# Scores as four row tiles of the matrix array, four single PSUM banks and two pairs

## The chip, the cores and the metric

One core of one Trainium2 chip. TensorE (PE) multiplies matrices out of SBUF into PSUM, eight banks of 128 partitions by 512 fp32; ScalarE (ACT) evaluates functions, VectorE (DVE) does elementwise work and reductions, GpSimd (POOL) the rest, and SyncE (SP) issues most DMAs. The metric is the device time of one execution in microseconds (us); lower is better.

## The reference

Input `x` is 2048 tokens of 448 features. Two branches read it and a sigmoid gate mixes them, everything in fp32:

```python
def _A_ref(x, wq, wk, wv, wo):                 # 16 heads of 28, one shared key and value
    q = (x @ wq).reshape(B, S, H, Dh).transpose(0, 2, 1, 3)
    k = x @ wk
    v = x @ wv
    scores = jnp.einsum("bhqd,bkd->bhqk", q, k) * (Dh ** -0.5)
    p = _softmax(scores, axis=-1)
    o = jnp.einsum("bhqk,bkd->bhqd", p, v)
    return o.transpose(0, 2, 1, 3).reshape(B, S, H * Dh) @ wo

def _B_ref(x, w1, w2, w3, w4):
    h = _gelu(_layernorm(x) @ w1)
    ...                                        # four column groups shifted by +1, -1, +2, -2 tokens
    x1 = x + hs @ w2
    return x1 + _gelu(_layernorm(x1) @ w3) @ w4

g = _sigmoid((x * gate_w).sum(-1, keepdims=True))
return g * a + (1 - g) * b
```

## The kernel before

The order of every engine's queue is written out by hand (a manual schedule): each engine runs its instructions in program order and waits on semaphores. Three stages follow one another.

**Stage 1 and 2 (first 401 us).** Projections to queries, keys, values (`stage_q`, `stage_kv`; they go through the DRAM tensor `qd`), the token mixer (`stage_w1`, `stage_w2`) and the MLP (`w3_part`, `w4_part`), each product made of two or three fp32r products of a high and a low half. `split_k` (L334) builds the keys for the attention on POOL. The last MLP product of the last block is left to the attention stage (`w4_job`, L835).

**Stage 3, attention.** It runs over 16 units `u` (four blocks of 512 queries by four groups of four heads). A unit has 16 key tiles `kt` of 128 keys. For each `kt` and head `j`, one matmul (L901) makes the scores of 128 keys by 512 queries in one PSUM bank: its 98 contraction rows are three stacked products of 32 rows (high q with high k, low q with high k, high q with low k, so that the sum is nearly fp32) and two rows that subtract a bound on the maximum. ACT reads the bank, writes `p = exp(scale * scores)` to SBUF (L903). Seven banks rotate for the scores (`bank`), the eighth holds the values: `pv_group` (L863) multiplies four `p` tiles by `vext` (values and a column of ones, 32 columns), each head in its own 32 columns of the array (`tile_position=(0, 32 * j)`, a column tile), and sums over a unit's 16 key tiles in that bank. These value products come in seven visits a unit (`VISITS`, L880), of two or three key tiles each; 22 `p` tiles (`PB`) bridge the time between.

**Around it.** `max_part` (L206) takes the scores of 32 keys of the next unit in four small matmuls, DVE their maximum (L211); `max_end` puts it as rows beside the queries by four small DMAs. `q_rows` (L192) copies the halves of a later unit's queries into the 98-row layout by three DMAs. `sums_begin`, `recip` and `norm` divide a finished unit by its sums, which go through DRAM to be spread over partitions (L780, L789, L791, L796). `wo_job` (L805) multiplies the result by `wo`, three matmuls of 448 columns for each 128 tokens, and DVE adds it to the output (L824). `pump` (L852) issues one matmul of a job at written places between the scores. After the last unit a tail divides by way of transposes on PE and checks that all sums are in range; else a block `redo` (not taken) computes everything with full maxima.

Of the kernel before, what the change touches and what calls it, by code (L numbers as in the profile page):

```python
# [16 lines left out]
P = 128  # L17
S = 2048
D = 448
# [12 lines left out]
PB = 22  # L32
# [9 lines left out]
def gated_mix_kernel(  # L42
# [25 lines left out]
    identR = keep.tile([P, P], F32R, name="identR")  # L68
    nc.vector.tensor_copy(identR, ident)
    x1 = keep.tile([P, NT, D], F32, name="x1")  # L70
    kS = keep.tile([P, S], F32R, name="kS")
# [14 lines left out]
    nc.gpsimd.memset(f32(kS)[96:128, :], 1.0)  # L86
# [4 lines left out]
    def misc_tile(name):  # L91
        return psA.tile([P, 512], F32, tag="misc", bufs=1, name=name)

# [85 lines left out]
    qs_of = [None, None]  # L179

    def q_load(u, raw):
        b, g = divmod(u, NG)
        qr_of[u] = raw
        nc.sync.dma_start(raw[0:4 * DH], qd[g, 0:4 * DH, 512 * b:512 * b + 512])

    def q_split(u, qh, ql):
        qr = qr_of.pop(u)[0:4 * DH]
        qh_of[u], ql_of[u] = qh[0:4 * DH], ql[0:4 * DH]
        nc.vector.tensor_copy(qh_of[u], qr)
        nc.vector.tensor_sub(ql_of[u], qr, f32(qh_of[u]))  # L190

    def q_rows(u):  # L192
        q_of[u] = qs_of[u % 2]
        for r, part in enumerate((qh_of[u], ql_of[u], qh_of[u])):
            nc.sync.dma_start(f32(q_of[u])[32 * r:32 * r + DH], f32(part))

    NU = NB * NG
    q_of = {}
    qr_of, qh_of, ql_of = {}, {}, {}
    mx_of = {}  # L200
    mc_of = {}

    def max_tile(name):
        return psA.tile([P, 512], F32, tag="mx", bufs=1, name=name)

    def max_part(u, t, tile_of):  # L206
        if t == 0:
            mx_of[u] = late.tile([P, 4, 4], F32, tag="mr", bufs=2, name=f"mr_{u}")
        ps = tile_of(f"m_{u}_{t}")[:, 0:4 * MK].rearrange("p (j k) -> p j k", j=4)
        nc.tensor.matmul(ps, qh_of[u][:, t * P:(t + 1) * P], khd[0:4 * DH], start=True, stop=True)  # L210
        nc.vector.reduce_max(mx_of[u][:, :, t], ps, axis=AX.X)  # L211

    def max_full(u, tile_of):
        mr = late.tile([P, 4, 4], F32, tag="mr", bufs=2, name=f"mf_{u}")
        for j in range(4):
            for t in range(4):
                mk = late.tile([P, NB], F32, tag="mk", bufs=2, name=f"mk_{u}_{j}_{t}")
                for kb in range(NB):
                    ps = tile_of(f"mf_{u}_{j}_{t}_{kb}")
                    nc.tensor.matmul(ps, q_of[u][0:96, j, t * P:(t + 1) * P], kS[0:96, kb * 512:kb * 512 + 512],  # L220
                                     start=True, stop=True)
                    nc.vector.reduce_max(mk[:, kb:kb + 1], ps, axis=AX.X)
                nc.vector.reduce_max(mr[:, j, t:t + 1], mk, axis=AX.X)
        mx_of[u] = mr

    def max_end(u):
# [7 lines left out]
        for p in range(4):  # L234
            nc.sync.dma_start(f32(qs_of[u % 2])[96:98, :, :].rearrange("k j (t p q) -> k p (j t) q", p=4, q=32)[:, p],
                              mrow[32 * p:32 * p + 32, :])
# [4 lines left out]
    with tc.tile_pool(name="s1b", bufs=1) as s1b, \  # L241
# [80 lines left out]
        kf_of = {}  # L322

        def stage_kv(b):
            cols = slice(512 * b, 512 * b + 512)
            kf = s1b.tile([96, 512], F32, tag="kf", bufs=2, name=f"kf_{b}")
            for r in range(3):
                for g in range(2):
                    nc.sync.dma_start(kf[32 * r + 16 * g:32 * r + 16 * g + 16, :], qd[g, 4 * DH:P, cols])
            for g in range(2):  # L330
                nc.sync.dma_start(vT[32 * b + 16 * g:32 * b + 16 * g + 16, :], qd[2 + g, 4 * DH:P, cols])
            kf_of[b] = kf

        def split_k(b):  # L334
            cols = slice(512 * b, 512 * b + 512)
            kf = kf_of[b]
            nc.gpsimd.tensor_copy(kS[0:96, cols], kf)
            nc.gpsimd.tensor_tensor(kS[64:96, cols], kf[64:96, :], f32(kS)[64:96, cols], ALU.subtract)
# [207 lines left out]
        split_k(0)  # L546
# [14 lines left out]
        split_k(1)  # L561
# [3 lines left out]
        split_k(2)  # L565
# [4 lines left out]
        khd = late.tile([P, 4, MK], F32R, name="khd")  # L570
        qh0 = late.tile([P, 512], F32R, tag="qh0", bufs=1, name="qh0")
        qs_of[0] = late.tile([P, 4, 512], F32R, name="qs0")
# [8 lines left out]
        def load_w34(i, pool):  # L581
            w3h.append(pool.tile([P, 4, 2 * P], F32R, name=f"w3h_{i}"))
            w3l.append(pool.tile([P, 4, 2 * P], F32R, name=f"w3l_{i}"))
            last = late if 2 * i + 2 == NF else pool
            w4h.append(last.tile([P, 2, D], F32R, name=f"w4h_{i}"))
            w4l.append(last.tile([P, 2, D], F32R, name=f"w4l_{i}"))
# [46 lines left out]
        split_k(3)  # L633
# [10 lines left out]
    with tc.tile_pool(name="s2", bufs=1, reuse_waits="tile") as s2, \  # L644
# [5 lines left out]
        fills = [lambda t=t: max_part(0, t, max_tile if t % 2 else misc_tile) for t in range(4)]  # L650
# [6 lines left out]
        def w3_part(b, f):  # L657
# [3 lines left out]
            if (b, f) == (NB - 1, NF - 1):  # L661
                gh = late.tile([P, 512], F32R, tag="qh0", bufs=1, name="gh_late")
                gl = late.tile([P, 512], F32R, name="gl_late")
            else:
                gh = s2.tile([P, 512], F32R, tag="gh", bufs=3, name=f"gh_{b}_{f}")
                gl = s2.tile([P, 512], F32R, tag="gl", bufs=3, name=f"gl_{b}_{f}")
            gf = s2.tile([P, 512], F32, tag="gf", bufs=2, name=f"gf_{b}_{f}")
# [14 lines left out]
        for b in range(NB):  # L682
            acc = [ps2.tile([P, 512], F32, tag="acc", bufs=4, name=f"acc_{b}_{t}") for t in range(4)]
            gs = {}
            for f in range(NF):
# [24 lines left out]
                if b == 1 and f == 1:  # L710
                    for z in (khd, qs_of[0][0:96]):
                        nc.gpsimd.memset(f32(z), 0.0)
                    for j in range(4):
                        nc.sync.dma_start(f32(khd)[j:4 * DH:4, j, :], f32(kS)[0:DH, 0:MK])
                    q_load(0, s2a.tile([P, 512], F32, tag="xn", bufs=1, name="qr_0"))
                if b == 1 and f == 5:
                    q_split(0, qh0, s2.tile([P, 512], F32R, tag="gl", bufs=3, name="ql_0"))
                    q_rows(0)
# [9 lines left out]
            if b == NB - 1:  # L728
                last_g = gs[NF - 1]
# [9 lines left out]
    with tc.tile_pool(name="s3", bufs=1, reuse_waits="tile") as s3, \  # L739
            tc.tile_pool(name="ps3", bufs=1, space=PSUM, reuse_waits="tile") as ps3:  # L740
        woh = s3.tile([P, 4, D], F32R, name="woh")
        wol = s3.tile([P, 4, D], F32R, name="wol")

        banks = [mm_tile("bank_0"), mm_tile("bank_1"), misc_tile("bank_2")]
        banks += [ps3.tile([P, 512], F32, name=f"bank_{i}") for i in range(3, 7)]
# [6 lines left out]
        qs_of[1] = s3.tile([P, 4, 512], F32R, name="qs1")  # L752
        nc.gpsimd.memset(f32(qs_of[1])[0:96], 0.0)
        def q_fetch(u):
            if u < NU:
                q_load(u, s3.tile([P, 512], F32, tag="qr", bufs=1, name=f"qr_{u}"))

        def q_begin(u):
            q_split(u, s3.tile([P, 512], F32R, tag="qh", bufs=2, name=f"qh_{u}"),
                    s3.tile([P, 512], F32R, tag="ql", bufs=1, name=f"ql_{u}"))  # L760

        q_fetch(1)
        q_begin(1)
        q_rows(1)
        q_fetch(2)
# [10 lines left out]
        def sums_begin(u, pv):  # L776
            o = s3.tile([P, 512], F32, tag="o", bufs=2, name=f"o_{u}")
            nc.vector.tensor_copy(o, pv)  # L778
# [15 lines left out]
        def norm(u, o, rb):  # L794
            on = s3.tile([P, 512], F32, tag="onf", bufs=2, name=f"on_{u}")
            nc.vector.tensor_mul(on, o, rb)  # L796
            onh = s3.tile([P, 512], F32R, tag="onh", bufs=2, name=f"onh_{u}")
            onl = s3.tile([P, 512], F32R, tag="onl", bufs=2, name=f"onl_{u}")
# [294 lines left out]
```

## Time and profile before

| | us |
|---|---|
| median of 3 runs | 957.31 (957.10 to 958.02) |
| profiled execution, span from the first to the last instruction | 957.7 |
| first score exp to the end of the last one | 401.5 to 943.3 |
| ACT busy, whole span | 648.2 |
| exps (L903): 1024, mean of one | 511.4 busy, 0.639 |

A matmul's recorded time contains the way through the array, which the next matmul overlaps; likewise an ACTIVATE's recorded time overlaps the next. So the pace of a stream is read from the distance of the starts, not from the mean duration, and a busy share of 99% says little about PE. In a row of the timeline, the first number is the start, the second the time until the last of the merged instructions ends; the bracket is the idle time of the engine before, and what ended it.

### The profile page before, as it was taken

Reading aid. Unit: us, or ns where it says so; the run is one execution under the profiler, and the core shown is the slowest. Engines: PE = TensorE matmul, PEld = TensorE weight load, DVE = VectorE, ACT = ScalarE, POOL = GpSimd, SP = SyncE. Lnnn points to the kernel's source line nnn. Section 1 sums busy time; section 2 is a strip of 40 time slices with the busy share of each in tenths; the row PEclk is TensorE's granted clock in tenths of the full one; section 3 lists DMA queues with packets and bytes.
Section 4 is the critical chain, followed back from the end, with each engine's and each line's share of the span. In section 5 each row is a group of like instructions: output and inputs, shape, how many; then the busy total and the mean of one; then the engine's idle time right before and its main releaser. Section 6 shows DMA issues by size and latency. Waiting matters only on the chain.

```text
span 957.7 us, 13557 instructions
## 1 busy us (share of the span) xinstructions
PE 948.7 (99%) x5187; PEld 631.2 (66%) x5187; DVE 278.7 (29%) x573; ACT 648.2 (68%) x1266; POOL 115.9 (12%) x139
## 2 busy tenths in 40 slices
PE   9999999999999999999999999999999999999996
PEld 6788888888888888755555555455555555545544
DVE  4664364532423411221222112122121222212112
ACT  5532444332222222499999999999999999999994
POOL 3344300200001410040000000000000000000000
PEclk9999999999999999999999999999999999999999
DMA  9823552201300300111011021011111101210101
GB/s 312 274 70 76 144 165 83 80 14 29 83 1 1 83 1 10 28 54 48 21 42 42 22 79 52 27 26 51 52 51 40 51 13 40 80 51 9 35 13 42
DMA packets 45319, 57.33 MB, mean 60 GB/s; under 512 B 9856, under 2 KB 28096, under 8 KB 45248
## 3 DMA queue, kind: packets, MB, share of 16 engines
q1 hardware_dynamic: 42224, 50.93, 18.4%
q10 hardware_dynamic: 3024, 5.47, 1.5%
q8 instruction: 42, 0.69, 0.3%
q14 instruction: 29, 0.24, 0.1%
HBM read 32.19 MB, written 11.67 MB: 46 GB/s over the span
## 4 chain that ended last, share of the span: by engine, by line
PE 98%; DMA 1%; DVE 0%; ACT 0%; issue 0%; SPq 0%; ACTq 0%
PE bank L901 28%; PE pv L870 25%; PE acc L678 5%; PE acc L680 5%; PE acc L679 5%; PE g L134 4%; PE g L135 4%; PE g L136 4%; PE bank L816 1%; PE bank L814 1%; PE bank L812 1%; PE g L137 1%; PE g L138 1%; PE h L134 1%; PE h L135 1%; PE h L136 1%
## 5 line engine op out<-in xcount | busy, mean ns | idle before, releaser
L903 ACT ACTIVATE p<-bank 128x512 f32<-128x512 f32 x1024 | 511.4, 639 | 33.1 <-PE bank L901 30.7
L901 PE MATMUL bank<-qs,kS 98*128 98x512 f32 x1024 | 305.8, 410 | 0.0
L901 PEld LDWEIGHTS bank<-qs,kS 98*128 98x128 f32 x1024 | 184.1, 189 | 134.3 <-issue 93.1
L870 PE MATMUL pv<-p,vext 128*32 128x512 f32 x2048 | 243.1, 598 | 0.0
L668 ACT ACTIVATE gh<-g 128x512 fp32r<-128x512 f32 x55 | 32.9, 598 | 183.6 <-PE g L138 183.6
L870 PEld LDWEIGHTS pv<-p,vext 128*32 128x32 f32 x2048 | 58.9, 109 | 114.9 <-issue 108.0
L670 DVE TENSOR_TENSOR gl<-gf,gh 128x512 fp32r<-128x512 f32 x55 | 38.2, 695 | 163.6 <-ACT gf L669 159.3
L678 PE MATMUL acc<-w4h,gh 128*128 128x448 f32 x220 | 80.2, 365 | 0.0
L680 PE MATMUL acc<-w4h,gl 128*128 128x448 f32 x220 | 80.0, 364 | 0.0
L679 PE MATMUL acc<-w4l,gh 128*128 128x448 f32 x220 | 79.8, 363 | 0.0
L824 DVE SCALAR_TENSOR_TENSOR ot<-bank,gg,ot 128x448 f32<-128x448 f32 x44 | 30.0, 684 | 146.9 <-ACT p L903 95.1
L799 POOL CAST onh<-on 128x512 fp32r<-128x512 f32 x15 | 9.2, 611 | 471.8 <-DVE on L796 471.8
L134 PE MATMUL g<-ah,w3h 128*128 128x512 f32 x168 | 65.8, 392 | 0.0
L135 PE MATMUL g<-al,w3h 128*128 128x512 f32 x168 | 65.7, 391 | 0.0
L136 PE MATMUL g<-ah,w3l 128*128 128x512 f32 x168 | 65.7, 391 | 0.0
L211 DVE TENSOR_REDUCE mr<-bank 128x4 f32<-128x128 f32 x60 | 17.6, 293 | 108.5 <-PE bank L210 108.5
L678 PEld LDWEIGHTS acc<-w4h,gh 128*128 128x128 f32 x220 | 41.3, 188 | 4.2
L679 PEld LDWEIGHTS acc<-w4l,gh 128*128 128x128 f32 x220 | 41.3, 188 | 4.2
L680 PEld LDWEIGHTS acc<-w4h,gl 128*128 128x128 f32 x220 | 41.3, 188 | 3.1
L778 DVE COPY o<-pv 128x512 f32<-128x512 f32 x15 | 10.4, 692 | 99.4 <-PE pv L870 99.4
L136 PEld LDWEIGHTS g<-ah,w3l 128*128 128x128 f32 x168 | 31.5, 188 | 7.0
L135 PEld LDWEIGHTS g<-al,w3h 128*128 128x128 f32 x168 | 31.5, 188 | 5.7
(196 smaller groups left out, 965.5 us busy)
## 6 DMA issues: line engine op xcount, KB each, us to landing
qs<-qh SPq DMA_DIRECT2D x32, 224.0 KB
qd<-qf ACTq DMA_DIRECT2D x16, 256.0 KB
rb<-rd SPq DMA_DIRECT2D x15, 256.0 KB
x<-in_x_dram SPq DMA_DIRECT2D x4, 896.0 KB
xd<-xt SPq DMA_DIRECT2D x16, 224.0 KB
w34raw<-in_w_dram SPq DMA_DIRECT2D x7, 512.0 KB
qr<-qd SPq DMA_DIRECT2D x16, 224.0 KB
qs<-ql SPq DMA_DIRECT2D x16, 224.0 KB
```

The costliest lines, as they stand in the source:

```text
L134: nc.tensor.matmul(ps, wh[:, c, :], ah[:, c, :], start=(c == 0), stop=False)
L135: nc.tensor.matmul(ps, wh[:, c, :], al[:, c, :], start=False, stop=False)
L136: nc.tensor.matmul(ps, wl[:, c, :], ah[:, c, :], start=False, stop=False)
L668: nc.scalar.activation(gh, ps, AF.Gelu_apprx_tanh)
L670: nc.vector.tensor_sub(gl, gf, f32(gh))
L678: nc.tensor.matmul(ps, gh[:, tok], w4h[i][:, k, :], start=(f == 0), stop=False)
L679: nc.tensor.matmul(ps, gh[:, tok], w4l[i][:, k, :], start=False, stop=False)
L680: nc.tensor.matmul(ps, gl[:, tok], w4h[i][:, k, :], start=False, stop=(f == stop))
L824: nc.vector.scalar_tensor_tensor(ot_of[n], ps, gg[:, n:n + 1], before, op0=ALU.mult, op1=ALU.add)
L870: nc.tensor.matmul(pv[32 * j:32 * j + 32, :], vext[:, kt, :], ps[j], start=(kt == 0), stop=(kt == NT - 1), tile_position=(0, 32 * j))
L901: nc.tensor.matmul(ps, kS[0:98, kt * P:(kt + 1) * P], q_of[u][0:98, j, :], start=True, stop=True)
L903: nc.scalar.activation(p, ps, AF.Exp, scale=SCALE)
```

## The change

- **Layout.** Queries and keys of head `j` now lie in rows 32j to 32j+31. The 98-row layouts (`kS`, `qs`) and the DMAs of `q_rows` go; the keys' halves are `kh` and `kl`, all four copies split on POOL in one go before the last `stage_w2`. A query unit is loaded by four DMAs in place of one, its maximum rows are written by eight in place of four.
- **Scores.** `scores` issues, for a key tile, three rounds of four matmuls of 32 rows: in a round each head uses its own 32 rows of the array (`tile_position=(32 * j, 0)`, a row tile) and its own bank. That is twelve matmuls of 32 rows in place of four of 98.
- **Banks.** Four single banks and two pairs of banks. The loop now goes over chunks of two key tiles. Heads 0 and 1 of a key tile get single banks, heads 2 and 3 a pair. ACT reads four single banks (512 columns each); the second pair by one exp of 1024 columns. The first pair is copied raw to SBUF by one DVE copy of 1024 columns, and ACT's last exp of the chunk (1024 columns) runs in place in SBUF.
- **Values.** The values of a chunk's two key tiles are made one chunk later, in the first single bank that this chunk's exps free, as an accumulation of two; DVE adds it to a sum in SBUF in each chunk (`values_end`). The output and last MLP products take the second single bank, one job a chunk in chunks 4 to 7 of a unit, as plain fp32 in four column tiles of 32 tokens (`by_columns`), without halves; so the splits of `wo` and of the results on POOL go. The next unit's maximum takes that bank in chunk 3, one reduction in place of four.
- **Last MLP tile.** One Gelu in place of two and no low half; `gf` has one buffer in place of two.
- **Tail.** The last unit's sum is added on DVE, the low halves go.

```diff
-PB = 22
+PB = 6
...
+    def scores(u, kt, ps):
+        kh = kh_of[0]
+        keys = slice(kt * P, (kt + 1) * P)
+        for r, (k, q) in enumerate(((kh, qh_of[u]), (kh, ql_of[u]), (kl, qh_of[u]))):
+            for j in range(4):
+                h = slice(32 * j, 32 * j + 32)
+                nc.tensor.matmul(ps[j], k[h, keys], q[h, :], start=(r == 0), stop=(r == 2), tile_position=(32 * j, 0))
...
-        split_k(0)
...
-        split_k(3)
+        for b in range(NB):
+            split_k(b)
...
-        banks = [mm_tile("bank_0"), mm_tile("bank_1"), misc_tile("bank_2")]
-        banks += [ps3.tile([P, 512], F32, name=f"bank_{i}") for i in range(3, 7)]
+        singles = [mm_tile("bank_0"), mm_tile("bank_1"), misc_tile("bank_2"), max_tile("bank_3")]
+        pairs = [ps3.tile([P, 2, 512], F32, name=f"pair_{i}") for i in range(2)]
...
+        def by_columns(ps, a, t, w):
+            for i in range(4):
+                c = t * P + 32 * i
+                nc.tensor.matmul(ps[32 * i:32 * i + 32, :], a[:, c:c + 32], w, start=True, stop=True,
+                                 tile_position=(0, 32 * i))
...
-                for j in range(4):
-                    n, at = 4 * k + j, 4 * kt + j
-                    ps = bank(f"s_{n}")
-                    nc.tensor.matmul(ps, kS[0:98, kt * P:(kt + 1) * P], q_of[u][0:98, j, :], start=True, stop=True)
-                    p = s3.tile([P, 512], F32, tag="p", bufs=PB, name=f"p_{n}")
-                    nc.scalar.activation(p, ps, AF.Exp, scale=SCALE)
-                    p_of[k].append(p)
-                    if at in pump_at:
-                        pump()
...
+        for c in range(NU * NT // 2 + 1):
+            u, i = divmod(c, NT // 2)
+            k = 2 * c
+            s0, s1, s2, s3_ = singles if c % 2 == 0 else singles[2:] + singles[:2]
+            if u < NU:
+                pa = score_tiles(u, 2 * i, s0, s1, pairs[0])
+                exps(pa, left, s0.unsqueeze(1))
+                exps(pa, right, s1.unsqueeze(1))
+                nc.vector.tensor_copy(pa[:, both], pairs[0])
+                pb = score_tiles(u, 2 * i + 1, s2, s3_, pairs[1])
+                exps(pb, left, s2.unsqueeze(1))
+                exps(pb, right, s3_.unsqueeze(1))
+                exps(pb, both, pairs[1])
+                exps(pa, both)
+            if c:
+                v = divmod(c - 1, NT // 2)[0]
+                pv = s0
+                values(k - 2, pv, True, False)
+                values(k - 1, pv, False, True)
+                if (v, i) != (NU - 1, 0):
+                    values_end(v, pv)
+                if i == 0 and v < NU - 1:
+                    sums.append(sums_begin(v))
+            if u == NU:
+                break
+            if i == 1 and sums:
+                norms.append(recip(*sums.pop()))
+            if i == 3 and norms:
+                w = norms[0][0]
+                norm(*norms.pop())
+                jobs += [lambda bank, w=w, t=t: wo_job(w, t, bank) for t in range(4)]
+            if i == 3 and u + 1 < NU:
+                max_part(u + 1, range(4), s1)
+                max_end(u + 1)
+            elif i > 3 and jobs:
+                jobs.pop(0)(s1)
```

339 lines of the change are left out of this document (136 added, 203 removed).

## The prediction

> **What bounds the kernel now.** I read the page's busy times first, then the windows by stage, then the waits, then timelines of single engines. PE is busy everywhere by its records; ACT is the other full engine, from the eighteenth slice on:
>
> ```profile
> PE 948.7 (99%) x5187; PEld 631.2 (66%) x5187; DVE 278.7 (29%) x573; ACT 648.2 (68%) x1266; POOL 115.9 (12%) x139
> ACT  5532444332222222499999999999999999999994
> ...
> 401.50:943.30 541.80, 541.80 (x3311) 286.30 (x3313) 109.81 (x260) 511.36 (x1024) 39.61 (x36) 1.00 0.15 41
> ...
> ACT p L903 <- PE bank L901: 30.7, 34, 2.7
> ...
> L903 ACT ACTIVATE p<-bank 128x512 f32<-128x512 f32 x1024 | 511.4, 639 | 33.1 <-PE bank L901 30.7
> ```
>
> The third line is the attention from its first exp to the end of its last, 541.8 us (PE, PEld, DVE, ACT, POOL); the change lies almost wholly there. The fourth line says that ACT waited 34 times for scores, 30.7 us in all. ACT's own pace, from its timeline:
>
> ```profile
> 401.97 13.33 ACT L903 ACTIVATE p<-bank 128x512 f32<-128x512 f32 x27
> ...
> 413.43 1.87 ACT L903 ACTIVATE p<-bank 128x512 f32<-128x512 f32 x3
> ...
> 603.21 26.14 ACT L903 ACTIVATE p<-bank 128x512 f32<-128x512 f32 x52 [0.98 <-PE bank L901]
> 630.20 5.99 ACT L903 ACTIVATE p<-bank 128x512 f32<-128x512 f32 x12 [0.85 <-PE bank L901]
> 637.15 1.09 ACT L903 ACTIVATE p<-bank 128x512 f32<-128x512 f32 x2 [0.96 <-PE bank L901]
> ```
>
> The 25th exp of the first row starts at 413.43: (413.43 - 401.97) / 24 = 0.477 us an exp without a wait. A unit of 64 exps needs 30.6; from 603.21 to 637.15, one unit, 33.94 pass. So ACT works 1024 x 0.477 = 488.8 of 541.8 us and stands still for 53, mostly while PE makes values. PE, from its timeline:
>
> ```profile
> 599.90 2.78 PE L870 MATMUL pv<-p,vext 128*32 128x512 f32 x24
> 602.61 2.13 PE L901 MATMUL bank<-qs,kS 98*128 98x512 f32 x8
> 604.67 0.64 PE L870 MATMUL pv<-p,vext 128*32 128x512 f32 x4
> ...
> L870 PE MATMUL pv<-p,vext x2048: 592/592/617, 404.5 to 944.3; 128*32 128x512 f32 x187
> ...
> 110.48 0.60 PE L343 MATMUL vp<-ident,vT 128*128 128x128 f32 x4
> ...
> L343 PE MATMUL vp<-ident,vT 128*128 128x128 f32 x4 | 0.6, 273 | 0.0
> ...
> 126.75 0.39 PE L134 MATMUL g<-ah,w3h 128*128 128x512 f32 x1
> 127.45 0.39 PE L134 MATMUL g<-ah,w3h 128*128 128x512 f32 x1
> ```
>
> Four column-tiled value matmuls of 0.62 end within 0.64, so they run together, and a group of four takes (2.78 - 0.59) / 5 = 0.43. An fp32r matmul of 512 columns takes 0.70 / 3 = 0.233 (L134, three apart). In a unit PE has 64 x 0.233 + 16 x 0.43 = 21.8 us of scores and values in 33.9: it isn't full. What costs is the order: in a visit of 2.7 us PE makes no scores, and seven banks of exps last no longer.
>
> **The change part by part.**
>
> *ACT's floor.* A chunk had eight exps, 3.82. It gets four of 512 (1.91), one of 1024 from PSUM, one of 1024 from SBUF. The nearest rows are casts of both widths:
>
> ```profile
> L125 ACT CAST ahk<-xkv 128x1024 fp32r<-128x1024 f32 x4 | 4.0, 1048 | 1.0 <-DMA xkv<-in_xT_dram 0.6 <-ACT qf L297 0.5
> L125 ACT CAST ahk<-xkv 128x512 fp32r<-128x512 f32 x4 | 2.5, 618 | 3.0 <-DMA xkv<-in_xT_dram 3.0
> ...
> 21.42 2.52 ACT L125 CAST ahk<-xkv 128x1024 fp32r<-128x1024 f32 x3 [0.45 <-ACT qf L297]
> ```
>
> 512 more columns cost 0.430, so 0.907 from PSUM. From SBUF: two of 1024 and one of 512 in 2.52, (2.52 - 0.618) / 2 = 0.951. Sum 1.909 + 0.907 + 0.951 = 3.77, only 0.05 less than before; 128 chunks are 482.2. The gain must come from the waits.
>
> *PE's work in a chunk.* The unknown is a round of four row tiles. Lower bound 0.233: each row tile still streams 512 columns and loads 128 columns of weights. If the weight loads went one after another, the transposes of line 343 bound them: (0.60 - 0.27) / 3 = 0.11 a load with its short matmul, 0.44 a round. Upper bound 4 x 0.233 = 0.93, no overlap at all. I take 0.233, since four column tiles do run together. Six rounds are 1.40, two groups of values 0.87. Changes of tile mode: after six groups from 599.90 the next would start at 602.50, the first score stands at 602.61; eight scores from there at 0.233 put the last at 604.24 where 602.61 + 2.13 - 0.39 gives 604.35; that one is followed at 604.67, 0.32 instead of 0.233 later. Together 0.31 a chunk. Jobs: four column tiles of 448, 0.375, in half of the chunks, 0.19. The maximum, below, 0.14 a chunk. PE 2.9 of 3.77, so ACT is the bound by 0.86.
>
> *Hand-offs.* From the start of a pass ACT starts its six exps at 0, 0.48, 0.95, 1.43, 1.91, 2.82. A bank is free 0.64 after its exp's start (L903's mean); then 0.23 to the first round, 0.47 to the third, 0.49 to the exp (602.61 and 603.21 above, less 0.11 for the unhidden load).
> - Next chunk's first key tile needs the fourth bank: 1.43 + 0.64 + 0.23 + 0.47 + 0.49 = 3.26, due at 3.77: 0.5 to spare.
> - Its second needs the pair: 1.91 + 1.07 + 1.19 = 4.17, due at 4.72.
> - Values wait for the exp at 3.77 to free the bank: start 4.6, done 5.66; DVE's add 0.70 (L778) to 6.4, a job's addition 0.68 (L824) to 7.1; the scores that need these banks are ready at 7.1 + 1.19 = 8.3, due at 2 x 3.77 + 0.95 = 8.5. 0.2 to spare, the tightest.
>
> ```profile
> L778 DVE COPY o<-pv 128x512 f32<-128x512 f32 x15 | 10.4, 692 | 99.4 <-PE pv L870 99.4
> L128 DVE TENSOR_TENSOR alk<-xkv,ahk 128x1024 fp32r<-128x1024 f32 x3 | 3.7, 1243 | 7.0 <-ACT ahk L125 6.7 <-ACT ahk L292 0.3
> L824 DVE SCALAR_TENSOR_TENSOR ot<-bank,gg,ot 128x448 f32<-128x448 f32 x44 | 30.0, 684 | 146.9 <-ACT p L903 95.1 <-PE bank L816 47.7 <-PE bank L812 4.1
> L211 DVE TENSOR_REDUCE mr<-bank 128x4 f32<-128x128 f32 x60 | 17.6, 293 | 108.5 <-PE bank L210 108.5
> L210 PE MATMUL bank<-khd,qh x60: 221/224/228, 410.8 to 887.1; 112*128 112x128 f32 x60
> L796 DVE TENSOR_TENSOR on<-o,rb x15: 649/650/693, 446.7 to 922.0; 128x512 f32<-128x512 f32 x15
> L787 DVE RECIPROCAL rr<-rt x15: 245/246/246, 439.6 to 915.5; 128x16 f32<-128x16 f32 x15
> L235 SPq DMA_DIRECT2D qs<-mrow x64: 610/624/714, 285.2 to 890.5; - x64
> 192.84 0.53 SPq L184 DMA_DIRECT2D qr<-qd  x1
> 399.44 2.42 DVE L734 TENSOR_TENSOR x<-x,acc 128x448 f32<-128x448 f32 x4 [1.23 <-PE acc L680]
> ```
>
> DVE's copy of the pair, about 1.24 (L128), brings DVE to 1.24 + 0.70 + 0.34 = 2.3 a chunk; covered, and due only at 2.82 of the pass.
>
> *Once a unit.* In chunk 3 four small matmuls (up to 0.23 each, two mode changes) stand before the scores, and DVE does norm (0.65), one reduction of 512 columns (0.29 + 0.4) and three small steps; the bank comes back about 0.7 later than with a job, 0.5 beyond the spare. Norm waits for sums that took up to 446.7 - 439.6 = 7.1 us by way of DRAM (L787 to L796), now placed two chunks, 7.5, behind: 0 to 1 us of waiting, I take 0.3. So 0.8 x 15 = 12. Everything behind it on DVE (reduction, pair copy, adds) is late with it. SP: eight maximum rows at 0.62 (L235) and four query loads at 0.53 (L184), 7 us of a 30 us unit; the rows are due at the unit's end and issued from its middle.
>
> *Once.* The second pair sits on accumulators that DVE frees at 399.44 + 2.42 = 401.86: second key tile at 403.1 instead of 402.4, 0.6. Key splits on POOL: four copies of 1.9 from 112.08 end near 119.8, the memsets behind them move from 116.0 to there; the first product that reads them starts at 126.75 (above). Without that cover, 4 us. One `gf` buffer: VectorE's 0.69 must end before the next Gelu, which PE's eleven products of a tile (11 x 0.233 = 2.6) cover. Tail: four low halves of 0.28 go, mode changes come; 0, bounds -1 and +1.
>
> ```profile
> 112.08 0.61 POOL L337 CAST kS<-kf 96x512 fp32r<-96x512 f32 x1
> 112.76 1.29 POOL L338 TENSOR_TENSOR kS<-kf,kS 32x512 fp32r<-32x512 f32 x1
> 116.04 0.81 POOL L110 MEMSET w3h<- 64x256 f32 x3
> ...
> L955 DVE TENSOR_TENSOR onl<-bank,onh 128x128 fp32r<-128x128 f32 x4 | 1.1, 282 | 0.1
> ```
>
> *Sum.* 957.7 - 541.8 + 482.2 + 12 + 0.6 = 910.7, against this execution's own 957.7, which is 0.4 above the median of the runs shown. I say 911.
>
> The Trainium skill (TensorE: Matmul & The Clock Gate, Part 3) reports 3.07 times the speed for four row tiles together; by it a round would be 4 x 0.233 / 3.07 = 0.30, PE 3.3 a chunk, and the sum the same. No row here has a row tile; it only makes the upper bound unlikelier.
>
> **The rivals.**
>
> *Row tiles overlap by half or less: slower.* Place: L203's rounds. PE's chunk is six rounds + 1.53 and becomes the bound; it equals the present 541.8 / 128 = 4.23 at a round of 0.45, the point from which the change loses. Two tiles at a time, 0.466: 4.33 x 128 = 554, time 971; no overlap: 7.1 x 128 = 909, 1325. For: the array has 98 of 128 rows busy already, so nothing here proves four separate streams. Against: the column tiles.
>
> *Weight loads in turn.* 0.44 a round: 4.17 x 128 = 534, time 951. For: the 0.11 of line 343; against: loads of the column tiles are hidden as well.
>
> *PE's issue pace.* A chunk has some 69 matmuls and loads, before 36. The densest lasting stream is line 870's 48 in 2.6 us, 0.054 each: 69 x 0.054 = 3.74, level with ACT; with every hand-off then tight, about 4.0 a chunk, 512, time 940.
> The Trainium skill (the same page, "Wait — 56ns, not 53.3ns?") gives about 62 ns for a matmul if its decoding is left to microcode: were that so for loads too, 69 x 0.062 = 4.28 a chunk, time 964; line 870's rows lie under that pace, and so speak against it.
>
> *The change doesn't do what it says*: ACT's waits only move, to the values' bank (spare 0.2). Another 0.6 us of DVE or PE lateness there in every chunk makes it 4.15: 947, hardly a gain.
>
> **How the numbers follow.** ACT-bound at 911: 0.62, its own range 898 (no waits) to 930. Loads in turn, issue pace or waits that move, 930 to 955: 0.15. Within 0.2% (all that a measurement of this kernel can tell from no change), the same rivals a little dearer: 0.03. Row tiles overlapping by half or less, or a dearer issue pace: 0.20. So faster 0.77, same 0.03, slower 0.20. The range goes from 895, a little below the case without waits for a cheaper exp from SBUF, to 965, which takes in the rivals up to the dearest issue pace and leaves out most of the slow case.
>
> **What would show it.** Right: ACT's exps follow one another at 0.48, 0.91 and 0.95 with waits of about a microsecond once a unit; the four matmuls of a round start within some 0.03 us, rounds 0.23 apart; a unit takes 30.2 to 31.5. Wrong: rounds of 0.44 or more; ACT waiting for line 203 in every chunk; exps of 1024 columns dearer than 0.95; or the MLP's products held up between 116 and 130 us.

## The result, and the profile after

| | before | after |
|---|---|---|
| median, us (four runs each on one chip) | 957.49 | 963.48 (962.74 to 963.87) |
| ratio to before | | 1.0063 [1.0049, 1.0077] |
| profiled span | 957.7 | 961.7 |
| first score exp to the end of the last one | 401.5 to 943.3 | 401.8 to 944.6 |

The changed kernel is slower by 0.6%; 911 was forecast. Between the spans lie 4.0 us: the attention takes 1.0 more, the stretch behind its last exp 2.7 more, the start 0.35. The other 2 between the medians come from the execution of before that was profiled: in every run for which both are known, the device time is 1.75 to 1.95 above the span (963.59 and 961.7 in the profiled one of after), so a span of 957.7 belongs to some 959.5, 2 above the median (an estimate). Where in that span the 2 us lie isn't known. So the attention didn't become 47 us shorter, it stayed as it was, or grew by up to 3.

The page of the profile after, first the busy times, then groups of instructions (busy us and mean ns, then idle us before them):

```profile
PE 943.5 (98%) x7575; PEld 562.6 (59%) x7575; DVE 497.2 (52%) x766; ACT 634.2 (66%) x1005; POOL 80.9 (8%) x111
...
L843 ACT ACTIVATE p<-bank 128x512 f32<-128x512 f32 x512 | 269.9, 638 | 44.5 <-PE pair L203 37.7
L854 PE MATMUL bank<-p,vext 128*32 128x512 f32 x2048 | 247.6, 600 | 1.3
L870 DVE COPY p<-pair 128x1024 f32<-128x1024 f32 x128 | 156.0, 1219 | 18.6 <-PE pair L203 14.8
```

ACT still waits 44.5 us for scores ahead of its exps of single banks, more than before (33.1). The L854 line carries the answer: 2048 value matmuls. The code issues 16 units x 16 key tiles x 4 heads = 1024. Each of these fp32 matmuls in a column tile is two instructions on the chip. The line of before that the prediction quotes (L870, x2048) says the same. ACT's waits by cause, and then the whole attention as one window (busy PE, PEld, DVE, ACT, POOL):

```profile
ACT p L843 <- PE pair L203: 37.7, 71, 1.1
```

```profile
401.82:944.62 542.80, 534.77 (x5656) 218.69 (x5656) 327.60 (x454) 498.28 (x768) 3.35 (x3) 1.00 0.07 22
```

71 waits for the pair in 128 chunks: about one for each of the 64 chunks with a job. Where they stand is seen in ACT's timeline, around chunk 7 of a unit and chunks 0 and 1 of the next:

```profile
601.55 2.07 ACT L843 ACTIVATE p<-bank 128x512 f32<-128x512 f32 x4 [0.53 <-PE pair L203]
603.47 1.05 ACT L843 ACTIVATE p<-pair 128x1024 f32<-128x1024 f32 x1
604.38 1.09 ACT L843 ACTIVATE p<-p 128x1024 f32<-128x1024 f32 x1
605.99 2.07 ACT L843 ACTIVATE p<-bank 128x512 f32<-128x512 f32 x4 [0.52 <-PE pair L203]
...
609.76 2.10 ACT L843 ACTIVATE p<-bank 128x512 f32<-128x512 f32 x4
...
613.53 2.15 ACT L843 ACTIVATE p<-bank 128x512 f32<-128x512 f32 x4
```

From 605.99 to 609.76 and on to 613.53, chunks without a job, ACT runs without a gap: 3.77, the forecast floor. From 601.55 to 605.99, chunk 7, which has a job, it is 4.44. The pitch of all chunks, worked out from the starts of their first exps (mean over units 1 to 14, us):

```
chunk of the unit        0     1     2     3     4     5     6     7    unit
after                  3.78  3.76  3.76  4.28  5.07  4.45  4.46  4.47   34.0
```

Three chunks keep ACT's floor, five don't; a unit takes 34.0, as before. What PE does in the chunk of 4.44 is in its timeline (one row of several that start together is shown for the second and third round):

```profile
600.50 0.50 PE L203 MATMUL bank<-qh,kh 32*128 32x512 f32 x2
...
600.84 0.39 PE L203 MATMUL bank<-ql,kh 32*128 32x512 f32 x1
...
601.07 0.39 PE L203 MATMUL pair<-qh,kl 32*128 32x512 f32 x1
...
601.44 0.50 PE L203 MATMUL pair<-qh,kh 32*128 32x512 f32 x2
...
601.78 0.39 PE L203 MATMUL pair<-ql,kh 32*128 32x512 f32 x2
...
602.01 0.39 PE L203 MATMUL pair<-qh,kl 32*128 32x512 f32 x2
602.33 1.92 PE L854 MATMUL bank<-p,vext 128*32 128x512 f32 x16
604.08 0.94 PE L812 MATMUL bank<-wof,on 128*32 128x448 f32 x8
604.94 0.50 PE L203 MATMUL bank<-qh,kh 32*128 32x512 f32 x2
```

Two key tiles of values are 16 instructions, four groups of four, and hold PE from 602.33 to 604.08: 1.75 us where the prediction had 0.87. A job is eight instructions and holds it for 0.86, change of mode included, where it had 0.375. The starts follow one another by 0.34, 0.23, 0.37, 0.34, 0.23, 0.32, 1.75, 0.86: PE is full but for about 0.13 ahead of 601.44. That bit is the second key tile waiting for its banks; DVE's timeline names it, the job's addition ends at 601.39:

```profile
599.94 0.69 DVE L786 TENSOR_TENSOR o<-o,bank 128x512 f32<-128x512 f32 x1 [1.60 <-PE bank L854]
600.70 0.69 DVE L828 SCALAR_TENSOR_TENSOR ot<-bank,gg,x 128x448 f32<-128x448 f32 x1
```

The same count turns the reading of before. The windows view of its unit (the first number with an x counts PE's matmuls):

```profile
603.21:637.15 33.94, 33.94 (x210) 18.01 (x209) 7.08 (x17) 31.97 (x65) 1.89 (x2) 1.00 0.14 37
```

64 scores, 64 values, 12 of jobs and 4 of the maximum would be 144; 208 and two neighbours are there because the values are 128. So 16 key tiles cost 16 x 0.86 = 13.8, not 6.9, and with 64 x 0.233 = 14.9, 12 x 0.205 = 2.5 and seven visits' changes of mode at 0.31 = 2.2 they make 33.4 of the 33.9: PE was full, and ACT's waits were only where that surfaced. The starts in the trace say the same: in the whole attention, 401 to 943 us, no matmul of before starts more than 0.52 after the one ahead of it, which is a group of four (0.43) and a change of mode (0.09).

### The profile page after: what moved, and what is told of

Same layout as the page of the kernel before. It is cut to its first block, busy times and chain, and to the rows that moved or that the text cites. A ratio compares the mean times of both kernels' runs of the same rounds, so it can differ in the third digit from the quotient of the medians.

```text
span 961.7 us, 18356 instructions
## 1 busy us (share of the span) xinstructions
PE 943.5 (98%) x7575; PEld 562.6 (59%) x7575; DVE 497.2 (52%) x766; ACT 634.2 (66%) x1005; POOL 80.9 (8%) x111
## 3 DMA queue, kind: packets, MB, share of 16 engines
q1 hardware_dynamic: 37304, 40.27, 13.8%
## 4 chain that ended last, share of the span: by engine, by line
PE 76%; ACT 18%; DVE 3%; issue 2%; DVEq 0%
ACT p L843 18%; PE bank L854 16%; PE bank L203 12%; PE bank L812 5%; PE acc L682 5%; PE acc L684 5%; PE acc L683 5%; PE g L135 4%; PE g L136 4%; PE g L137 4%; PE hs L460 1%; PE pair L203 1%; PE hs L461 1%; PE g L138 1%; PE g L139 1%
## 5 line engine op out<-in xcount | busy, mean ns | idle before, releaser
L843 ACT ACTIVATE p<-bank 128x512 f32<-128x512 f32 x512 | 269.9, 638 | 44.5 <-PE pair L203 37.7
L854 PE MATMUL bank<-p,vext 128*32 128x512 f32 x2048 | 247.6, 600 | 1.3
L870 DVE COPY p<-pair 128x1024 f32<-128x1024 f32 x128 | 156.0, 1219 | 18.6 <-PE pair L203 14.8
L203 PE MATMUL bank<-qh,kh 32*128 32x512 f32 x512 | 143.9, 480 | 7.2 <-DVE mr L212 5.1
L843 ACT ACTIVATE p<-p 128x1024 f32<-128x1024 f32 x128 | 144.1, 1126 | 0.0
L843 ACT ACTIVATE p<-pair 128x1024 f32<-128x1024 f32 x128 | 139.6, 1091 | 0.0
L854 PEld LDWEIGHTS bank<-p,vext 128*32 128x32 f32 x2048 | 53.8, 109 | 128.1 <-issue 77.6
L203 PE MATMUL pair<-qh,kh 32*128 32x512 f32 x512 | 128.1, 496 | 0.3 <-DVE x L738 0.3
L203 PE MATMUL bank<-ql,kh 32*128 32x512 f32 x512 | 122.5, 397 | 0.0
L203 PE MATMUL bank<-qh,kl 32*128 32x512 f32 x512 | 118.6, 390 | 0.0
L203 PE MATMUL pair<-qh,kl 32*128 32x512 f32 x512 | 101.4, 391 | 0.0
```

The lines of the kernel that those rows point to most:

```text
L203: nc.tensor.matmul(ps[j], k[h, keys], q[h, :], start=(r == 0), stop=(r == 2), tile_position=(32 * j, 0))
L843: nc.scalar.activation(p[:, heads], p[:, heads] if source is None else source, AF.Exp, scale=SCALE)
L854: nc.tensor.matmul(pv[32 * j:32 * j + 32, :], vext[:, kt, :], p[:, j], start=first, stop=last, tile_position=(0, 32 * j))
L870: nc.vector.tensor_copy(pa[:, both], pairs[0])
```

## The experiments

Theory 1 at the start: value matmuls cost double, and this fills PE. The rivals put the loss on the hand-off of banks by DVE, on the place of the jobs, or on the order of the visits. The pitches of all variants of the changed kernel stand in one table behind the last experiment.

**Values at the size that the prediction had.** Exps are written as bf16, the values as a high and a low bf16 half, two groups of four of 0.22 each for a key tile. (The raw copy of the first pair, which stays fp32, gets a tile of its own; that part of the edit isn't shown.)

```diff
-            p_of[u * NT + kt] = p = s3.tile([P, 4, 512], F32, ...)
+            p_of[u * NT + kt] = p = s3.tile([P, 4, 512], mybir.dt.bfloat16, ...)
...
-            for j in range(4):
-                nc.tensor.matmul(pv[32 * j:32 * j + 32, :], vext[:, kt, :], p[:, j],
-                                 start=first, stop=last, tile_position=(0, 32 * j))
+            for r, v in enumerate((vh, vl)):
+                for j in range(4):
+                    nc.tensor.matmul(pv[32 * j:32 * j + 32, :], v[:, kt, :], p[:, j],
+                                     start=first and r == 0, stop=last and r == 1, tile_position=(0, 32 * j))
```

> Leaves out part of the precision: the exps are written as bf16 and multiplied by the values as two bf16 halves (high, low), so that the value products of a key tile take two groups of 512 columns in one pass each, 0.43 us, the size that the prediction gave them, in place of the four passes that the trace of the changed kernel shows (0.86). Theory 1 (the value products were counted at half their size, everything else in the chunk is as predicted): PE's chunk with a job becomes 6 x 0.23 + 0.31 + 0.87 + 0.75 = 3.3, under ACT's 3.77; chunks of 3.77 everywhere but after the maximum, unit 30.5 to 31, time 905 to 918. Rival (the rounds of row tiles or the hand-offs of banks are what is too long): chunks with a job stay above 4.2, time above 945.

Measured: 909.22 (908.11 to 909.95), ratio 0.949 [0.9475, 0.9506]. PE's timeline in that kernel, the values of one chunk, and from its page the group of single exps:

```profile
601.99 0.40 PE L860 MATMUL bank<-p,vh 128*32 128x512 bf16 x4
602.21 0.39 PE L860 MATMUL bank<-p,vl 128*32 128x512 bf16 x4
602.43 0.39 PE L860 MATMUL bank<-p,vh 128*32 128x512 bf16 x4
602.64 0.39 PE L860 MATMUL bank<-p,vl 128*32 128x512 bf16 x4
602.86 0.93 PE L812 MATMUL bank<-wof,on 128*32 128x448 f32 x8
```

```profile
L848 ACT ACTIVATE p<-bank 128x512 bf16<-128x512 f32 x512 | 304.9, 912 | 0.4 <-PE bank L203 0.4
```

Four groups now take 602.86 - 601.99 = 0.87 us, exactly the prediction's term, and ACT's wait ahead of these exps falls from 44.5 to 0.4 us. The time is the forecast 911 less 2. This one term carries the miss. That the sum is met so closely is luck in part: the attention takes 488.9 (402.45 to 891.39) where 494.8 was forecast, since the once-a-unit loss is 0.46 and not 0.8, while the start is 1.0 and the end 1.8 longer than before, and device time is 1.8 above the span.

**Jobs' products alone, and jobs' additions alone.** The first multiplies 64 of 448 columns in the loop's jobs (six sevenths of these products are left out), the second adds 64 of 448 columns on DVE, in place in `x1` (six sevenths of these additions are left out).

```diff
-                nc.tensor.matmul(ps[32 * i:32 * i + 32, :], a[:, c:c + 32], w, start=True, stop=True,
+                nc.tensor.matmul(ps[32 * i:32 * i + 32, 0:n], a[:, c:c + 32], w[:, 0:n], start=True, stop=True,
```

```diff
-            nc.vector.scalar_tensor_tensor(ot_of[n], ps, gg[:, n:n + 1], before, op0=ALU.mult, op1=ALU.add)
+            nc.vector.scalar_tensor_tensor(ot_of[n][:, 0:64], ps[:, 0:64], gg[:, n:n + 1], before[:, 0:64],
+                                           op0=ALU.mult, op1=ALU.add)
```

> Leaves out work: the output and last MLP products of the main loop have 64 of 448 columns; the additions of DVE stay whole (they read old scores beyond). Theory 1 (PE's own work sets a chunk with a job): chunk 4.45 minus about 0.6 = 3.85, 62 such chunks, time 963.5 - 37 = 926 (920 to 932). Rival (DVE's addition holds the bank that the next scores need): the addition starts after the add of the values as before and frees the bank no earlier, chunk 4.3 or more, time 952 or more.

> Leaves out work: DVE's additions of the jobs take 64 of 448 columns; the products on PE stay whole. Theory 1: only the wait of about 0.15 before the second key tile's scores goes, chunk 4.45 to 4.3, time 953 (950 to 957). Rival (DVE's addition sets the chunk): chunk 3.8, time 922.

Measured: products short 950.31, ratio 0.9917 [0.9901, 0.9934]; additions short 956.41, ratio 0.9985 [0.9975, 0.9994]. The first misses theory 1's 926 by far and lies just under the rival's 952; the second is inside theory 1's range. With short products, chunks 5 to 7 only go from 4.45 to 4.28, and chunk 0 rises from 3.78 to 4.16. DVE's timeline of that kernel, and PE's:

```profile
599.79 0.69 DVE L786 TENSOR_TENSOR o<-o,bank 128x512 f32<-128x512 f32 x1 [0.81 <-PE bank L812]
600.40 0.68 DVE L828 SCALAR_TENSOR_TENSOR ot<-bank,gg,x 128x448 f32<-128x448 f32 x1
```

```profile
599.47 0.29 PE L812 MATMUL bank<-wof,on 128*32 128x64 f32 x8
599.70 0.50 PE L203 MATMUL bank<-qh,kh 32*128 32x512 f32 x2
...
600.26 0.40 PE L203 MATMUL bank<-qh,kl 32*128 32x512 f32 x2
...
601.13 0.50 PE L203 MATMUL pair<-qh,kh 32*128 32x512 f32 x2
...
602.02 1.92 PE L854 MATMUL bank<-p,vext 128*32 128x512 f32 x16
```

The short product holds PE for 0.23 (599.47 to 599.70) in place of 0.86 and is done early, but its addition stands behind that of the values on DVE and ends at 601.08. The second key tile needs that bank: its round at 601.13 instead of 600.49 is 0.64 late, where it was 0.13 late before, and most of what PE gained goes into that. With short additions the second key tile isn't held. PE's timeline, and the row of ACT's that the next values wait for:

```profile
601.54 0.94 PE L812 MATMUL bank<-wof,on 128*32 128x448 f32 x8
602.41 0.50 PE L203 MATMUL bank<-qh,kh 32*128 32x512 f32 x2
...
602.98 0.39 PE L203 MATMUL bank<-qh,kl 32*128 32x512 f32 x2
...
603.21 0.39 PE L203 MATMUL bank<-qh,kh 32*128 32x512 f32 x2
...
603.67 0.39 PE L203 MATMUL bank<-qh,kl 32*128 32x512 f32 x1
...
604.11 1.47 PE L854 MATMUL bank<-p,vext 128*32 128x512 f32 x9
```

```profile
603.46 2.06 ACT L843 ACTIVATE p<-bank 128x512 f32<-128x512 f32 x4 [0.39 <-PE pair L203]
```

The second key tile follows at 603.21, 0.23 behind the last round of the first. But PE isn't full there either: the values start 0.44 behind the last round, at 604.11, not 0.32, since they are made in the bank that the exp at 603.46 reads for 0.64.

So theory 1 was too simple. PE's own work in such a chunk is about 4.2: the 4.44 less 0.13 of waiting, and less 0.11 because the second key tile's first round takes 0.23 without that pause, not 0.34. Three loops, each a little longer, close beside it (the values are 1.75 in all three):

- In the changed kernel, by the job's product: values, product 0.86, 0.20 until its addition starts, addition 0.69, 0.05 to the second key tile, its rounds 0.89: 4.44, measured 4.45. (The addition starts 0.76 behind that of the values; with the short product 0.61 are enough, so it is the product that it waits for.)
- With short products, by both additions: values, 0.32 until their addition starts, 0.61 to that of the job, 0.68, 0.05, rounds 0.89: 4.30, measured 4.28.
- With short additions, by the first exp: 1.05 from the first key tile's first round to that exp, 0.65 to the values, values, product 0.87: 4.32, measured 4.31.

Neither products nor additions can be shortened alone with much profit.

**Jobs spread over more chunks.** Each job as two halves of 224 columns, one half a chunk in chunks 4 to 7, 0 and 1, two in chunk 2.

```diff
-            elif i > 3 and jobs:
-                jobs.pop(0)(s1)
+            elif c:
+                for _ in range(2 if i == 2 or u == NU - 1 and i > 3 else 1):
+                    if jobs:
+                        jobs.pop(0)(s1)
```

> Same computation: each job in two halves of 224 columns, spread over chunks 4 to 7 and 0 to 2 of the next unit (two halves in chunk 2), instead of four whole ones in chunks 4 to 7. Theory 1 (a chunk takes the longer of PE's and ACT's work, and PE has 3.43 without a job, 4.2 with one): PE 3.43 + 0.38 = 3.8 to 3.95 in most chunks, about 4.4 in chunk 2, unit 32 to 32.5, time 963.5 - 16 x 1.7 = 936 (928 to 944). Rival (the sum of PE's work and its waits for ACT is what counts, wherever a job stands): 958 or more.

Measured: 980.07, ratio 1.023 [1.0213, 1.0247], far above theory 1's range and inside the rival's "958 or more", which has no upper end. A chunk with a half takes 4.05: it is the loop by both additions with 0.44 for the job's, 4.06. So the floor of 3.77 is lost in all eight chunks. Two halves in one chunk cost 5.5 to 5.7. DVE's timeline of a chunk 2 shows why:

```profile
620.84 0.69 DVE L786 TENSOR_TENSOR o<-o,bank 128x512 f32<-128x512 f32 x1 [1.75 <-ACT p L843]
621.44 0.44 DVE L828 SCALAR_TENSOR_TENSOR ot<-bank,gg,x 128x224 f32<-128x224 f32 x1
622.59 0.45 DVE L828 SCALAR_TENSOR_TENSOR ot<-bank,gg,x 128x224 f32<-128x224 f32 x1 [0.71 <-PE bank L812]
```

Both halves use one bank, so the second product waits until DVE has added the first (621.88; the product starts at 621.94), and PE, which works in program order, waits with it. Neither theory had named these two reasons.

**Products and additions both short.** The two edits above together; six sevenths of both are left out.

> The changed kernel with the jobs' products and the jobs' additions in the loop both on 64 of 448 columns; it leaves out six sevenths of both. Theory 1 (one loop closes in each chunk with a job: values, job, DVE's addition of the job, second key tile's rounds, next values; either part alone leaves the other path, PE's own work or the two additions in a row, at 4.3): with both short the path is 1.73 + 0.2 + 0.69 + 0.15 + 0.6 + 0.3 = 3.7, under ACT's 3.77; chunks 4 to 7 take 3.77 to 3.85, the time is 905 to 922. Rival (the two savings of 7.2 and 1.1 us only add, since something else near 4.3 limits these chunks): 945 to 951.

Measured: 926.72, ratio 0.9674 [0.9658, 0.969]: 36.8 us below the changed kernel, while the two edits alone saved 13.2 and 7.1. (The expectation's 7.2 and 1.1 are counted from the kernel before.) They don't just add, which the loops explain and the rival doesn't. Chunks 5 to 7 take 3.89, a little above the forecast 3.77 to 3.85, and the time misses 922: an addition of 64 columns still takes 0.28 us, not the 0.15 put in. With 0.28 the loop by both additions is 3.90.

**The values of before at half their length.** The kernel before with the same bf16 exps and halves, its scores untouched.

> The kernel before, its scores untouched (98 rows in one matmul a head), with exps written as bf16 and the values as a high and a low bf16 half, so that a key tile's values take 0.43 us instead of 0.86; the exps are rounded to bf16. Theory 1 (the kernel before was bound by PE, of whose 33.9 us a unit the values are 16 x 0.86 = 13.8; with half of them PE needs 27.0 and ACT's 64 x 0.477 = 30.5 is the bound): a unit of 30.6 to 31.2, time 905 to 915, so that row tiles with banks in pairs add next to nothing to it beside the 909 of the changed kernel with such values (the floors differ by 0.05 a chunk, 6 us). Rival (the order of the visits, not their length, makes ACT wait; only row tiles remove it): 935 or more.

Measured: 937.64, ratio 0.9789 [0.9772, 0.9805], by the number in the rival's range of 935 or more. But its first unit took 52.2 us, all others about 31.4, and nearly all of that first unit's excess is one wait. From the waits in that stretch:

```profile
PE pv L875 <- POOL vh L863: 19.8, 1, 19.8
```

The new split of the values stood in POOL's queue behind the split of `wo` and the weighing of `x1`. The next run moves it ahead of them.

> As e5, the kernel before with values of half the length, but the split of vext into its bf16 halves stands on POOL ahead of wo's split and of the weighing of x1. In e5 it stood behind them, and the first values waited once for it: 20.35 us in which ACT had no scores, in the first unit; its other units took 31.36. Theory 1 (before was bound by PE through the length of its values; the stall of e5 was its own doing): 937.6 - 20.4 = 917, 914 to 920, so that row tiles and pairs are worth some 9 us beside such values, of which the floors explain 6. Rival (the stall only moves to another wait of the first unit, or the visits still hold up ACT): 930 or more.

Measured: 916.37 (915.98 to 916.56), ratio 0.9565 [0.9549, 0.9581]; a unit 31.36. So halving the values' length there brings 41 us with no row tile. That run alone wouldn't part PE's total from the length of a single visit, since the edit halves both; PE's starts without a gap, above, show that it was the total. Row tiles, pairs and the new hand-offs beside such values are worth the last 7 (916.4 to 909.2).

**A fourth round of scores.** Low half of k by low half of q, 0.46 us more of row tiles a chunk.

```diff
-        for r, (k, q) in enumerate(((kh, qh_of[u]), (kh, ql_of[u]), (kl, qh_of[u]))):
+        for r, (k, q) in enumerate(((kh, qh_of[u]), (kh, ql_of[u]), (kl, qh_of[u]), (kl, ql_of[u]))):
```

> The changed kernel with a fourth round of scores (low half of k by low half of q) for each key tile: 0.46 us more of row tiles on PE a chunk and nothing else. Theory 1 (a round costs PE 0.23, and PE's own work is 3.43 in a chunk without a job and about 4.3 in one with): chunks without a job go from 3.77 to 3.9, with a job from 4.45 to 4.7 to 4.9; time 985 to 1005. Rival (the rounds hide behind the waits for DVE and ACT, PE isn't full): 963 to 975. Rival (a round costs more than 0.23 when they come in fours): above 1010.

Measured: 990.91, ratio 1.0345 [1.0328, 1.0362], inside theory 1's range. Chunks without a job now show PE's own work, 3.92; less the two rounds it was 3.46, 0.3 under ACT's floor. Chunks with a job went up by 0.23 only, to 4.68, and there no round waits any longer; less the two rounds that is 4.22, again PE's own work with a job.

**The exp table earlier, and the maximum in another chunk.** The first adds, to the kernel with half values, one exp of a single column behind the last Gelu.

```diff
+        early = s3.tile([P, 1], F32, name="early")
+        nc.scalar.activation(early, invE[:, 0:1], AF.Exp, scale=SCALE)
```

> The changed kernel with values of half the length (exps as bf16, values as two bf16 halves: 909.2 measured) and one exp of a single column placed behind the last Gelu, so that ACT's load of the exp table (1.28 us) no longer stands between the first scores and the first exp. Theory 1 (the load is late by waiting for the first scores and delays the whole attention by its length): 907.9, 907.4 to 908.4. Rival (the first exp waits for something else, too): 909.

Measured: 908.13 (907.00 to 908.49), ratio 0.9477 [0.9462, 0.9493]. ACT's timeline at the start of the attention, in the first kernel of half values, then in this one, and last the load in the kernel before:

```profile
401.16 1.28 ACT L848 ACT_TABLE_LOAD   x1 [5.75 <-PE bank L203]
402.45 1.08 ACT L848 ACTIVATE p<-bank 128x512 bf16<-128x512 f32 x2
```

```profile
395.65 1.28 ACT L841 ACT_TABLE_LOAD   x1
397.46 0.20 ACT L841 ACTIVATE early<-invE 128x1 f32<-128x1 f32 x1 [0.53 <-PE acc L684]
401.40 2.06 ACT L851 ACTIVATE p<-bank 128x512 bf16<-128x512 f32 x4 [3.74 <-PE bank L203]
```

```profile
397.50 1.28 ACT L903 ACT_TABLE_LOAD   x1
```

The load left the path, and the first exp starts 1.05 earlier. The median falls by 1.1, as forecast, but the intervals of the two kernels overlap, and the attention ends only 0.6 earlier (890.80 against 891.39), since the first unit takes 31.5 there and 30.1 without the early load. So that the time gained is the load's isn't shown.

The second moves the next unit's maximum from chunk 3 to chunk 2, away from `norm`: once in the kernel of half values, once in the changed kernel as it is.

```diff
-            if i == 3 and u + 1 < NU:
+            if i == 2 and u + 1 < NU:
                 max_part(u + 1, range(4), s1)
```

> The kernel of e8 (values of half the length, early exp table) with the next unit's maximum in chunk 2 instead of chunk 3. In e8 all chunks of a unit take 3.76 to 3.78 but chunk 4, 4.15. Theory 1 (norm and the maximum's reduction with its small steps in one chunk make VectorE late; one at a time is covered): chunk 4 falls to 3.8, 15 x 0.38 = 5.7 us less, 902.5, 901 to 904. Rival (norm alone, waiting for its sums from DRAM, makes VectorE late): 907 to 908.5.

> The changed kernel, values as they are (fp32), with the next unit's maximum in chunk 2 instead of chunk 3. Chunk 3 takes 4.28 there and chunk 4 5.05, against 3.77 without and 4.45 with a job: 0.5 and 0.6 more. Theory 1 (the second is VectorE's lateness, of norm and the reduction in one chunk; the first is PE's own time and the bank held by the reduction, and stays): 0.5 x 15 = 7 less, 956, 953 to 959. Rival (PE is full in these chunks, and the order on VectorE is of no account): 962 to 965.

Measured: 907.94, ratio 0.9477 [0.9461, 0.9493], no gain, and so theory 1's 901 to 904 is missed and the rival's range met: chunk 4 fell from 4.15 to 3.99, but chunks 5 to 7 rose by 0.03 to 0.05 each. The rival's reason isn't what the trace shows: `norm` runs there directly behind the addition of the values (598.71 and 599.32) with no wait for DRAM. What holds chunk 4 stays open. In the changed kernel it gave 952.98, ratio 0.9949 [0.9933, 0.9966], 10.5 us less, at the lower end of the forecast: the maximum's own 0.5 moved from chunk 3 to chunk 2, and chunk 4 fell from 5.07 to 4.39. DVE's timeline of the changed kernel shows what the move takes apart:

```profile
620.73 0.68 DVE L807 TENSOR_TENSOR on<-o,rb 128x512 f32<-128x512 f32 x1
621.33 0.68 DVE L212 TENSOR_REDUCE mr<-bank 128x16 f32<-128x512 f32 x1
...
622.60 1.18 DVE L870 COPY p<-pair 128x1024 f32<-128x1024 f32 x1
```

The maximum's bank stands behind `norm`, and the pair's copy behind both.

All pitches, each worked out as above:

```
chunk of the unit             0     1     2     3     4     5     6     7    unit
after                       3.78  3.76  3.76  4.28  5.07  4.45  4.46  4.47   34.0
half values                 3.76  3.76  3.76  3.78  4.20  3.77  3.76  3.77   30.6
job products short          4.16  3.78  3.76  4.23  4.43  4.28  4.28  4.30   33.2
job additions short         3.78  3.76  3.76  4.28  5.07  4.31  4.31  4.33   33.6
both short                  3.78  3.77  3.76  4.28  4.43  3.89  3.88  3.90   31.7
jobs spread                 4.06  4.06  5.52  4.16  4.68  4.09  4.05  4.05   34.7
fourth round                3.92  3.92  3.94  4.52  5.36  4.68  4.69  4.70   35.7
half values, early table    3.76  3.76  3.76  3.76  4.15  3.78  3.76  3.76   30.5
the same, maximum apart     3.78  3.76  3.76  3.76  3.99  3.81  3.81  3.81   30.5
maximum apart               3.78  3.76  4.23  3.78  4.39  4.45  4.46  4.47   33.3
```

Of the versions that leave no work out, those with half values and exps rounded to bf16 beat both kernels (908 to 909 in the changed kernel, 916 in the kernel before), and so does, with exps in fp32, the maximum in chunk 2 (953).

## Why the prediction was wrong

- **The step that failed** is the term "two groups of values 0.87" in PE's work of a chunk, and with it the job's 0.375. Both come from "a group of four takes (2.78 - 0.59) / 5 = 0.43", which is right for four instructions and was taken for a key tile. The row said x24 for a visit whose three key tiles have 12 matmuls in the code, and L870 x2048 where the code has 1024: a key tile is two groups, 0.86. Measured in the chunk above: 1.75 for 0.87, 0.86 for 0.375 and its part of the mode changes. PE's work with a job became about 4.2 instead of 1.40 + 0.87 + 0.31 + 0.375 = 2.96, and so passed ACT's 3.77; the loops through the same values made it 4.45. The Trainium skill (FP8 and Floating Point Precision, TensorE Precision Notes) says that true fp32 takes four passes through the array; the trace agrees, 0.86 is four times the 0.215 of one bf16 pass in the run with half values, and that rule could have caught the miscount.
- **"It isn't full. What costs is the order"** fell with the same count: PE's unit is 33.4 of 33.9, with no gap between its starts, and the run of before with half values gained 41 us from the values' length.
- **ACT's floor** was right: 3.77 forecast, 3.76 to 3.78 in all chunks that nothing holds.
- **Row tiles** were right: four matmuls start within 0.01 to 0.03 us, rounds follow at 0.23, the fourth ones too. The rivals of partial overlap and of loads in turn fell. So did the issue pace: the fourth round's chunk without a job issues 48 matmuls and 48 loads in 3.92 us, 0.041 each, under the 0.054 that the rival needed. The Trainium skill (TensorE: Matmul & The Clock Gate, Part 3) gives 3.07 times the speed for four row tiles; here four go in the time of one, 0.23.
- **Hand-offs**: the place was the right one, with the wrong duration in it. The prediction let the job's addition follow that of the values; with both products doubled it is the job's product that ends last. Values from 4.6 with 1.73, the job 0.75 and 0.2 from there to its addition end at 7.3; the addition ends at 8.0 and the second key tile's exps are ready at 9.2, due at 8.5. That is 0.7 late where "0.2 to spare" stood; measured, 4.45 - 3.77 = 0.68. The rival "waits only move" named this place, at a price of 0.6 in every chunk; it was 0.68 in the 64 that have a job. So ACT-bound chunks were forecast and loops through PE and DVE measured.
- **Once a unit**: 0.8 forecast, (4.28 - 3.77) + (5.07 - 4.45) = 1.13 measured, 17 us over 15 units in place of 12. `norm` never waited for its sums from DRAM (0.68 us, nothing idle ahead); the reduction took 0.68 as put in, but `norm`, reduction and pair copy came in one row.
- **Sum of the attention**: 64 x 0.68 = 43.5 from jobs and 17 - 12 = 5 from the maximum, 48.5 above the forecast 494.8, against 542.8 measured. The forecast's 910.7 is moreover a span; as a device time it would be about 1.8 more. The rivals' times aren't added up alike: 940 has the once-a-unit 12 in it, 947, 951 and 971 haven't, and the 1.53 in them is 1.51 by its terms.
- **Once**: key splits on POOL and the single `gf` buffer cost nothing that shows; the first scores even start at 398.93, and the 0.6 for the second pair didn't come: its rounds start at 400.51. The exp table's load (1.28) came into the path instead, unforeseen; before, it lay at 397.50, in time in which ACT waited anyway. The tail was put at 0, with +1 as bound, and took 2.7 more. Its four output products are column tiles too and count double, 0.86 each where three matmuls of 0.205 stood: 1.0 of it. The rest stays open.

## What to carry to other kernels

Before a pace is read out of a row, divide its count of instructions by the count that the code issues: the fp32 matmuls here were two instructions each, and a row's pace was half of what one costs. Where an engine's summed work comes to within a few per cent of the stage, that engine is the bound, wherever the waits surface. Where several paths through a loop have nearly one length, shortening one alone brings little (13 and 7 us here, 37 together); test them together.

## What the runs showed of the hardware

- An fp32 matmul of 512 columns in a column tile is recorded as two instructions: four column tiles side by side take 0.43 us for each of the two, 0.86 with both. With bf16 operands it is one, and the four take 0.22. In fp32 a key tile's values, for all their 32 columns, cost nearly as much as its four heads' scores in 98 rows (4 x 0.233 = 0.93).
- Four row tiles of 32 rows ran fully side by side, 0.23 us a round, with their weight loads hidden behind the round before; only the first round of a series, or behind a pause, takes 0.34.
- In the changed kernel ACT's table load stood behind the wait of the exp that needed it: idle for 5.75 us, and then 1.28 us of load with the scores already there. In the kernel before, the same load ran at 397.50, right behind the last Gelu, and the exp followed at 401.47. The traces differ in one thing there: in the changed kernel a separate instruction that waits for semaphores (394.18 to 400.50) stands ahead of the load, in the kernel before the exp's wait is part of the exp.
